# Retention and two MoE layers on one core: where raw weight tiles wait, and in which step a tile or a chunk's copy is handled

## The chip, the core and the metric

One core of a Trainium2 chip runs the kernel. The metric is the device time in microseconds of one execution; 1212.71 us is the median of 3 runs of the kernel before (1211.6 to 1213.98). The engines are TensorE (PE, with its weight loads as PEld), VectorE (DVE), ScalarE (ACT), GpSimd (POOL) and SyncE (SP, which here only issues transfers).

## The reference

```python
# retention: B, H, S, D = 4, 8, 768, 64
state = gamma * state + outer(k[t], v[t])      # per batch and head
y[t] = q[t] @ state / sqrt(D)
# x: 3072 tokens of 512 (all heads of a token side by side)
h = x @ w_in                                   # 512 -> 2048
P = a[0] + a[1]*h + a[2]*h**2 + a[3]*h**3
Q = 1 + abs(b[0])*abs(h) + abs(b[1])*h**2
x = (P / (Q + 1e-6)) @ w_out                   # 2048 -> 512
h = x @ w_in2
out = (h * clip(h + 3, 0, 6) / 6) @ w_out2
```

All is float32.

## The kernel before, in words

**Matmuls.** Each float32 operand is split into a high part that TensorE takes as it is and a low remainder, so each product is three passes: high by high, high by low, low by high. The 3072 tokens are 6 blocks of 512, the 2048 hidden columns 16 tiles of 128 (`f`). One step of the main loop (L657) is one block and one `f` of one layer: `emit_h` (L322) makes 12 matmuls into a PSUM tile `h`, and `emit_o` (L334) makes the 12 matmuls of the output for the step two before (`LAG`). There are 192 steps. Layer 0 (the rational function) begins with block 0, `f` 0 to 7 (steps 0 to 7, `CUT1`), then block 1 with all 16 `f` (steps 8 to 23), then block 0's other 8 (steps 24 to 31), then blocks 2 to 5.

**Between the matmuls.** For layer 0 each step holds, one step behind `h`, `s1_h` (ACT, L403 to 405), `s1_pq` (DVE, L411, 412, 415) and `s1_r` (ACT, L420 and 421), and two steps behind, `s1_g` (DVE, L426 to 428), `s_hi` (ACT, L433, the high part `gh`) and `s_lo` (DVE, L439, the low part `gl`). The output matmuls of a step wait for that step's `gh` and then its `gl`.

**Weights.** A weight tile is one job: 32 jobs for layer 0, in the order in which they are needed (`jobs`, L485). A job is a load of 512 KB by SP (`w_load`), a scaling on ACT (L116), three bit operations on DVE (`w_bits`, L124, 125, 128), the high part on ACT (L136), and the low part either by a POOL transfer that adds (jobs 3 to 25, with one more ACT copy, L140) or by a DVE subtraction (L148, jobs 26 to 31). `w_until(n)` (L500) says how many jobs are to be done after step n: a step does one or two until that number is reached. `w_ahead` (L509) issues loads as soon as a place is free. There are six places: two `raw` tiles and the four tiles in which the finished weights `wi14`, `wo14`, `wi15` and `wo15` will lie (`SPARE`); before, jobs from number 24 on may use the two `raw` tiles alone. Job 24 is `wo` of f = 11, and the last, 31, is `wo` of f = 15.

**Retention.** A block has 4 chunks of 128 tokens. `chunk_at` (L552) puts a chunk's parts into steps: the loads (SP, five transfers), `att_q` and `att_v` (DVE, L201 and 206), the scores (PE, L219), the mask (DVE, L228), the output `py` and the new state (PE, L250 to 276), and then `att_xh` (ACT, L306, or L301 for block 2, whose result goes through DRAM) and `att_evac` (DVE, L313 and 317). The lists `begin`, `before` and `after` say where in a step a part stands: `begin` ahead of `s1_g` and `s_hi`, `before` behind `s1_pq`, `after` behind the output matmuls. Block 1's chunks are worked in steps -1 to 7, block 2's (`VIA`) from step 8 on.

**Order.** Nothing is moved by a scheduler: each engine runs its instructions in the order in which the loop writes them, and waits in that order. SP's loads wait in their order too, each for its place.

```python
w_until:  4 + 2 * (n + 1) if n < CUT1 else 4 + 2 * CUT1 + n + 1 - CUT1
w_ahead:  rooms = [t for t in free if i < SPARE_TO or t not in SPARE]
w_first:  w_bits(job i); w_scale_next(i + 3); w_hi(job i)
loop:     emit_h, s1_h, begin, s1_g + s_hi, w_second, w_first,
          s1_pq with s_lo inside, s1_r, before, [w_second, w_first], w_ahead,
          emit_o, after
```

Of the kernel before, what the change touches and what calls it, by code (L numbers as in the profile page):

```python
# [18 lines left out]
VIA = 2  # L19
CUT1, CUT2 = 8, 8  # L20
LAG = 2
SUMS = ((3, 26), (32, 40))
EARLY_AT = 8
SPARE, SPARE_TO = ("wi14", "wo14", "wi15", "wo15"), 24
WARM = 3
Q_CONST = 1.0 + 1e-6
LN_SCALE = 2.0**16
# [4 lines left out]
def tile_retention_moe_moe2(  # L32
# [66 lines left out]
    def w_load(tag, kind, layer, f):  # L99
        src = ((w_in1, w_in2) if kind == "wi" else (w_out1, w_out2))[layer].bitcast(I32)  # L100
        raw = pair_tile(tag, f"r{kind}{layer}_{f}").bitcast(I32)
        if kind == "wi":
            nc.sync.dma_start(
                out=raw.rearrange("p (c f) -> p c f", c=KD),
                in_=src[:, f * 256 : (f + 1) * 256].rearrange("(c p) f -> p c f", p=128),
            )
        else:
            nc.sync.dma_start(out=raw, in_=src[f * 128 : (f + 1) * 128, :])
        raws[kind, layer, f] = raw.rearrange("p (n t) -> p n t", t=2)
# [212 lines left out]
    def emit_h(key):  # L322
        layer, blk, f = key
        ps = ps_h.tile([128, 512], F32, tag="h", name=f"h{layer}_{blk}_{f}")
        wh, wl = weights["wi", layer, f]
        xh, xl = xin[blk + layer * NBLK]
        pairs = ((wh, xh), (wh, xl), (wl, xh))
        for n, (i, c) in enumerate((i, c) for i in range(3) for c in range(KD)):
            w, x = pairs[i]
            cs = slice(c * 128, (c + 1) * 128)  # L330
            nc.tensor.matmul(ps, lhsT=w[:, cs], rhs=x[:, c, :], start=n == 0, stop=n == 3 * KD - 1)  # L331
        hps[key] = ps
# [41 lines left out]
    def emit_evac(layer, blk, f):  # L374
        earlier = partial.pop((layer, blk), None)
        for j, ps in enumerate(acc.pop((layer, blk))):
            scale = G_SCALE if layer == 0 else 1.0 / 6.0
            if earlier:
                o = earlier[j]
                nc.vector.scalar_tensor_tensor(out=o, in0=ps, scalar=scale, in1=o, op0=ALU.mult, op1=ALU.add)  # L380
            else:
                o = out_tile(layer, blk, j, f"o{layer}_{blk}_{f}_{j}")
                if layer == 0 or j % 2 == 0:
                    nc.scalar.activation(o, ps, AF.Copy, scale=scale)
                else:
                    nc.vector.tensor_scalar(out=o, in0=ps, scalar1=scale, scalar2=None, op0=ALU.mult)
            t0 = blk * NB + j * 128
            if layer == 0:
                to = x2_dram[blk][j]
            else:  # L390
                to = out[t0 : t0 + 128, :] if f == FT - 1 else part_dram[j]
            nc.sync.dma_start(out=to, in_=o)
# [31 lines left out]
    def s1_g(key):  # L424
        u, p, r = tm[key]
        nc.vector.scalar_tensor_tensor(out=u, in0=u, scalar=Q_CONST, in1=r, op0=ALU.add, op1=ALU.mult)  # L426
        nc.vector.scalar_tensor_tensor(out=p, in0=p, scalar=ab[:, 0:1], in1=r, op0=ALU.add, op1=ALU.mult)  # L427
        nc.vector.scalar_tensor_tensor(out=p, in0=u, scalar=-2.0 * LN_SCALE, in1=p, op0=ALU.add, op1=ALU.mult)  # L428
        tm[key] = p

    def s_hi(key):
        gh = g_p.tile([128, NB], F32R, tag="gh", name="gh" + "_".join(map(str, key)))
        nc.scalar.activation(gh, tm[key], AF.Copy)  # L433
        gsp[key] = gh

    def s_lo(key):
        gh = gsp[key]
        gl = g_p.tile([128, NB], F32R, tag="gl", name="gl" + "_".join(map(str, key)))
        nc.vector.tensor_tensor(out=gl, in0=tm.pop(key), in1=gh.bitcast(F32), op=ALU.subtract)  # L439
        gsp[key] = (gh, gl)  # L440
# [40 lines left out]
    def at_step(n):  # L481
        return steps[n] if 0 <= n < len(steps) else None


    jobs = []  # L485
    for layer in range(2):
        need = []
        for f in range(FT):
            n = min(at_of[layer, b, f] for b in range(NBLK))
            need += [(n, "wi", layer, f), (n + LAG, "wo", layer, f)]  # L490
        jobs += [j[1:] for j in sorted(need, key=lambda j: j[0])]
    NW = 2 * FT
    made = {"load": 0, "scale": 0, "bits": 0, "lo": 0}
    free = [*SPARE, "raw", "raw"]
# [5 lines left out]
    def w_until(n):  # L500

        if n < N1 - FT:
            return min(NW, 4 + 2 * (n + 1) if n < CUT1 else 4 + 2 * CUT1 + n + 1 - CUT1)
        m = n - N1
        if m < 0:
            return NW + (m + FT) // 2
        return min(2 * NW, NW + 7 + (135 * (m + 1) + 99) // 100 if m < CUT2 else NW + 11 + m)

    def w_ahead(lim):  # L509
        while made["load"] < lim:  # L510
            i = made["load"]
            rooms = [t for t in free if i < SPARE_TO or t not in SPARE]
            if not rooms:
                return
            held[i] = rooms[0]
            free.remove(rooms[0])
            w_load(held[i], *jobs[i])
            made["load"] += 1
# [8 lines left out]
    def w_first():  # L527
        i = made["bits"]
        if made["scale"] == i:
            w_ahead(i + 1)  # L530
            w_scale_next(i + 1)
        w_bits(*jobs[i])
        w_scale_next(i + 3)
        w_hi(*jobs[i])
        if by_dma(i):
            w_minus(*jobs[i])
        made["bits"] += 1
# [6 lines left out]
            made["lo"] += 1  # L544


    begin, before, after, begun = {}, {}, {}, []

    def put(where, n, fn, *args):
        where.setdefault(n, []).append((fn, *args))  # L550

    def chunk_at(blk, c, s, loads=None):  # L552
        if loads is not None:
            put(before, loads, att_load, blk, c)
        put(before, s - 1, att_q, blk, c)
        put(before, s - 1, att_v, blk, c)
        put(after, s, att_scores, blk, c)
        put(before, s + 1, att_mask, blk, c)
        put(after, s + 1, att_out, blk, c)
        put(begin, s + 2, att_xh, blk, c)  # L560
        put(before, s + 2, att_evac, blk, c)

    for c in range(CPB):
        chunk_at(1, c, 2 * c - 1, max(2 * c - 4, -1))
        chunk_at(VIA, c, CUT1 + 1 + 4 * c, CUT1 - 1 + 4 * c)
        for b in range(VIA + 1, NBLK):
            n0 = at_of[0, b - 1, 0] if b > VIA + 1 else 2 * FT
            chunk_at(b, c, n0 + 4 * c, n0 + 4 * c - 2)
    for key in (VIA, *range(NBLK, 2 * NBLK)):
        n = at_of[0, key, 0] if key < NBLK else at_of[1, key - NBLK, 0]  # L570
# [20 lines left out]
    att_load(0, 0, (3, 2))  # L591
    att_load(0, 1)
    w_ahead(1)
    att_load(0, 2)
    att_load(0, 3, (0, 4, 1, 3))
# [51 lines left out]
    att_evac(0, 3)  # L647
    w_second()
    w_first()
    for parts in (begin, before, after):  # L650
        for n in sorted(n for n in parts if n < 0):
            for fn, *args in parts.pop(n):
                if fn is not att_load:
                    begun.append((fn, *args))

    late = []
    for n in range(len(steps) + LAG):  # L657
        cur, k1, k2 = (at_step(n - i) for i in range(3))
        todo = w_until(n) - made["bits"]
        if cur:  # L660
            emit_h(cur)
        for fn, *args in begun:
            fn(*args)
        begun.clear()
        if k1:
            (s1_h, s2_h)[k1[0]](k1)
        for key in late:
            if key[:2] not in partial and key[0] == 0:
                emit_evac(*key)
        for fn, *args in begin.get(n, ()):  # L670
            fn(*args)
        if k2 and k2[0] == 0:
            s1_g(k2)
            s_hi(k2)
        elif k2:
            s_lo(k2)
        for key in late:
            if key[:2] in acc:
                emit_evac(*key)
        late.clear()  # L680
        while made["lo"] < made["bits"]:
            w_second()
        rest = (lambda: s_lo(k2)) if k2 and k2[0] == 0 else None
        if k1 and k1[0] == 1:
            if rest:
                rest()
            s2_g(k1)
            s_hi(k1)
        if todo > 0:
            w_first()  # L690
        if k1 and k1[0] == 0:
            s1_pq(k1, rest)
            s1_r(k1)
        if todo > 1:
            w_second()
        for fn, *args in before.get(n, ()):
            fn(*args)
        if n == N1 - FT:
            free += ["kv", "T"]
        if todo > 1:  # L700
            w_first()
        w_ahead(NW if n < N1 - FT else 2 * NW)
        if n == 1:
            w_scale_next(NW)
        o = at_step(n - LAG)
        if o:
            emit_o(o)
            if o[2] == ends[o][1]:
                late.append(o)
        for fn, *args in after.get(n, ()):  # L710
            fn(*args)
        if cur and cur[1:] == (0, FT - 1):
            sum_load(*cur[:2])
# [71 lines left out]
```

## Time and profile before

| | us |
|---|---|
| median of 3 runs | 1212.71 (1211.6 to 1213.98) |
| profiled execution, its own time | 1212.05 |
| its span, first to last instruction | 1210.1 |
| PE busy / DVE busy / ACT busy | 1158.3 / 805.6 / 624.5 |
| mean granted TensorE clock | 0.984 of full |

The profiled execution lies 0.66 us under the median. In the span, steps 0 to 191 begin with their first `h` matmul; step 8 begins at 105.55 us, step 23 at 230.42 us. A busy share of PE says little, since matmuls overlap; the distance from one step's first `h` matmul to the next one's is the measure of pace.

### The profile page before, as it was taken

The numbers are of one execution on the slowest core, as the hardware profiler recorded it, in microseconds if no ns is written. First come the engines' busy times: TensorE is split into PE (matmuls) and PEld (weight loads), VectorE is DVE, ScalarE is ACT, GpSimd is POOL, SyncE is SP. The second block draws the span as 40 slices with busy tenths as digits, with TensorE's granted clock in tenths as the row PEclk, the third lists the DMA queues.
The fourth block names the chain that finished last, engine by engine and source line by source line (L and its number), as shares of the span: only waits on it lengthen the run. The fifth ranks groups of instructions, "written<-read, shape, count | busy, mean of one in ns | idle before, by whom it ended". The sixth has DMA issues, their size and how long they took to land.

```text
span 1210.1 us, 15716 instructions
## 1 busy us (share of the span) xinstructions
PE 1158.3 (96%) x6022; PEld 937.0 (77%) x6022; DVE 805.6 (67%) x1250; ACT 624.5 (52%) x1017; POOL 27.6 (2%) x37
## 2 busy tenths in 40 slices
PE   7687798999999999999999999999999999999998
PEld 5565676788888888888777788888888888888886
DVE  6899789999888788887899997643332232322222
ACT  2577666676666666756787765433222222322222
POOL 0112000000000000000000000000000000000000
PEclk9889999999999999999999999999999999999999
DMA  9877543032111311213233454202100100100000
GB/s 334 261 181 189 152 126 101 27 131 79 45 44 44 103 63 44 79 44 110 62 87 83 121 176 139 87 1 87 61 9 1 61 9 1 61 9 1 35 1 35
DMA packets 59115, 99.42 MB, mean 82 GB/s; under 512 B 5280, under 2 KB 23840, under 8 KB 59040
## 3 DMA queue, kind: packets, MB, share of 16 engines
q1 hardware_dynamic: 54576, 90.29, 22.6%
q0 software_dynamic: 4464, 8.13, 4.1%
q8 instruction: 47, 0.77, 0.3%
q14 instruction: 28, 0.23, 0.1%
HBM read 74.54 MB, written 15.73 MB: 75 GB/s over the span
## 4 chain that ended last, share of the span: by engine, by line
PE 74%; DVE 5%; ACT 2%; issue 1%; ACTq 0%; DVEq 0%
PE h L331 36%; PE accA L355 18%; PE accB L355 18%; PE sc L219 1%; PE py L250 1%; DVE u L426 1%; DVE u L412 1%; DVE p L411 1%; DVE p L427 1%; PE py L276 1%; ACT r L420 0%; ACT r L421 0%; DVE p L415 0%; PE py L262 0%; DVE p L428 0%
## 5 line engine op out<-in xcount | busy, mean ns | idle before, releaser
L331 PE MATMUL h<-xh,wi 128*128 128x512 f32 x1536 | 419.7, 395 | 0.7 <-ACT xh L306 0.7
L331 PEld LDWEIGHTS h<-xh,wi 128*128 128x128 f32 x1536 | 288.4, 190 | 65.4 <-issue 3.3
L331 PE MATMUL h<-xl,wi 128*128 128x512 f32 x768 | 207.5, 392 | 0.0
L451 DVE SCALAR_TENSOR_TENSOR g<-r,h 128x512 f32<-128x512 f32 x96 | 66.0, 688 | 164.5 <-ACT r L445 164.0
L331 PEld LDWEIGHTS h<-xl,wi 128*128 128x128 f32 x768 | 145.5, 189 | 31.4
L445 ACT ACTIVATE r<-h,cst 128x512 f32<-128x512 f32 x96 | 65.9, 687 | 178.0 <-PE h L331 177.5
L439 DVE TENSOR_TENSOR gl<-g,gh 128x512 fp32r<-128x512 f32 x96 | 66.5, 692 | 112.3 <-ACT gh L433 112.3
L433 ACT ACTIVATE gh<-g 128x512 fp32r<-128x512 f32 x96 | 60.8, 633 | 150.5 <-PE accB L355 116.5
L355 PE MATMUL accA<-gh,wo 128*128 128x512 f32 x384 | 121.5, 398 | 12.4 <-ACT gh L433 12.3
L355 PE MATMUL accB<-gh,wo 128*128 128x512 f32 x384 | 120.7, 396 | 0.0
L355 PE MATMUL accB<-wo,gh 128*128 128x512 f32 x384 | 118.2, 389 | 0.0
L355 PE MATMUL accA<-wo,gh 128*128 128x512 f32 x384 | 118.2, 389 | 0.0
L355 PEld LDWEIGHTS accA<-gh,wo 128*128 128x128 f32 x384 | 71.7, 190 | 31.9 <-ACT gh L433 17.4
L403 ACT ACTIVATE p<-h,ab 128x512 f32<-128x512 f32 x96 | 74.3, 774 | 39.0 <-PE h L331 36.4
L420 ACT ACTIVATE r<-u,cst 128x512 f32<-128x512 f32 x96 | 69.2, 721 | 42.2 <-DVE u L412 42.2
L439 DVE TENSOR_TENSOR gl<-p,gh 128x512 fp32r<-128x512 f32 x96 | 65.9, 686 | 32.9 <-ACT gh L433 32.7
L355 PEld LDWEIGHTS accB<-gh,wo 128*128 128x128 f32 x384 | 73.7, 192 | 15.8
L355 PEld LDWEIGHTS accA<-wo,gh 128*128 128x128 f32 x384 | 72.1, 188 | 15.0
L355 PEld LDWEIGHTS accB<-wo,gh 128*128 128x128 f32 x384 | 72.1, 188 | 14.9
L433 ACT ACTIVATE gh<-p 128x512 fp32r<-128x512 f32 x96 | 60.7, 632 | 34.9 <-DVE p L428 34.9
L355 PE MATMUL accA<-gl,wo 128*128 128x512 f32 x192 | 64.9, 414 | 14.3 <-DVE gl L439 14.3
L355 PE MATMUL accA<-wo,gl 128*128 128x512 f32 x192 | 74.7, 389 | 0.0
(74 smaller groups left out, 1477.3 us busy)
## 6 DMA issues: line engine op xcount, KB each, us to landing
rwi<-in_moe_w_in_dram SPq DMA_DIRECT2D x32, 512.0 KB, 4.4
rwo<-in_moe_w_out_dram SPq DMA_DIRECT2D x32, 512.0 KB, 4.1
T<-in_qk_t_dram SPq DMA_DIRECT2D x48, 256.0 KB, 4.2
kv<-in_kv_dram SPq DMA_DIRECT2D x32, 256.0 KB, 4.5
x<-o SPq DMA_DIRECT2D x24, 256.0 KB, 2.2
xr<-x SPq DMA_DIRECT2D x24, 256.0 KB, 3.6
out_dram<-o SPq DMA_DIRECT2D x20, 256.0 KB, 2.1
wi<-rwi POOLq DMA_DIRECT2D x17, 256.0 KB, 4.8
```

The lines of the kernel that those rows point to most:

```text
L219: nc.tensor.matmul(banks[e][:, p * CH : (p + 1) * CH], lhsT=kT[rows, p, :], rhs=qT[rows, p, :], start=True, stop=True)
L250: nc.tensor.matmul(to(e, j, i), lhsT=vr[:, 2 * p + e, :], rhs=am[:, e * NP + p, :], start=j == 0, stop=first and j == 1, skip_group_check= ...
L276: nc.tensor.matmul(to(e, j, i), lhsT=state[rows, p * D : (p + 1) * D], rhs=qT[rows, p, :], start=False, stop=j == 1, skip_group_check=True,)
L331: nc.tensor.matmul(ps, lhsT=w[:, cs], rhs=x[:, c, :], start=n == 0, stop=n == 3 * KD - 1)
L355: nc.tensor.matmul(acc[layer, blk][j], lhsT=l, rhs=r, start=f == f0 and i == 0, stop=f == f1 and i == 2)
L403: nc.scalar.activation(p, h, AF.Identity, scale=ab[:, 3:4], bias=ab[:, 2:3])
L411: nc.vector.tensor_tensor(out=p, in0=p, in1=h, op=ALU.mult)
L420: nc.scalar.activation(r, u, AF.Ln, scale=1.0 / LN_SCALE, bias=ln_bias)
L433: nc.scalar.activation(gh, tm[key], AF.Copy)
L439: nc.vector.tensor_tensor(out=gl, in0=tm.pop(key), in1=gh.bitcast(F32), op=ALU.subtract)
L445: nc.scalar.activation(r, hps[key], AF.Relu, bias=three)
L451: nc.vector.scalar_tensor_tensor(out=g, in0=r, scalar=6.0, in1=h, op0=ALU.min, op1=ALU.mult)
```

## The change

Four things change. The four spare tiles may hold a raw tile of any job that lies at least three jobs ahead of the weight that will live there (so jobs up to 24, 26, 27 and 28 in `wi14`, `wi15`, `wo14` and `wo15`), where before it was jobs up to 23 in all four. From step 8 on, `w_until` asks for four jobs in five steps instead of one in each: steps 8 to 19 did 13 jobs (two in step 8), now steps 8 to 22 do them, with none in steps 13 and 18. For blocks 1 and 2 `att_xh` stands in a new list `middle`, behind `s_hi`. Block 2's loads, scores, mask and output stand one step earlier, its `att_xh` and `att_evac` in the same step as before.

```diff
--- before.py
+++ after.py
@@ -21,7 +21,7 @@
 LAG = 2
 SUMS = ((3, 26), (32, 40))
 EARLY_AT = 8
-SPARE, SPARE_TO = ("wi14", "wo14", "wi15", "wo15"), 24
+SPARE = ("wi14", "wi15", "wo14", "wo15")
 WARM = 3
 Q_CONST = 1.0 + 1e-6
 LN_SCALE = 2.0**16
@@ -500,7 +500,7 @@
     def w_until(n):
 
         if n < N1 - FT:
-            return min(NW, 4 + 2 * (n + 1) if n < CUT1 else 4 + 2 * CUT1 + n + 1 - CUT1)
+            return min(NW, 4 + 2 * (n + 1) if n < CUT1 else 4 + 2 * CUT1 + 4 * (n + 1 - CUT1) // 5)
         m = n - N1
         if m < 0:
             return NW + (m + FT) // 2
@@ -509,7 +509,7 @@
     def w_ahead(lim):
         while made["load"] < lim:
             i = made["load"]
-            rooms = [t for t in free if i < SPARE_TO or t not in SPARE]
+            rooms = [t for t in free if t not in SPARE or i + 3 <= jobs.index((t[:2], 0, int(t[2:])))]
             if not rooms:
                 return
             held[i] = rooms[0]
@@ -544,7 +544,7 @@
             made["lo"] += 1
 
 
-    begin, before, after, begun = {}, {}, {}, []
+    begin, middle, before, after, begun = {}, {}, {}, {}, []
 
     def put(where, n, fn, *args):
         where.setdefault(n, []).append((fn, *args))
@@ -557,12 +557,14 @@
         put(after, s, att_scores, blk, c)
         put(before, s + 1, att_mask, blk, c)
         put(after, s + 1, att_out, blk, c)
-        put(begin, s + 2, att_xh, blk, c)
+
+        s += blk == VIA
+        put(middle if blk <= VIA else begin, s + 2, att_xh, blk, c)
         put(before, s + 2, att_evac, blk, c)
 
     for c in range(CPB):
         chunk_at(1, c, 2 * c - 1, max(2 * c - 4, -1))
-        chunk_at(VIA, c, CUT1 + 1 + 4 * c, CUT1 - 1 + 4 * c)
+        chunk_at(VIA, c, CUT1 + 4 * c, CUT1 - 2 + 4 * c)
         for b in range(VIA + 1, NBLK):
             n0 = at_of[0, b - 1, 0] if b > VIA + 1 else 2 * FT
             chunk_at(b, c, n0 + 4 * c, n0 + 4 * c - 2)
@@ -647,7 +649,7 @@
     att_evac(0, 3)
     w_second()
     w_first()
-    for parts in (begin, before, after):
+    for parts in (begin, middle, before, after):
         for n in sorted(n for n in parts if n < 0):
             for fn, *args in parts.pop(n):
                 if fn is not att_load:
@@ -674,6 +676,8 @@
             s_hi(k2)
         elif k2:
             s_lo(k2)
+        for fn, *args in middle.get(n, ()):
+            fn(*args)
         for key in late:
             if key[:2] in acc:
                 emit_evac(*key)
```

SP's queue around the load of job 24 (`rwo_11`; `rwi_f` and `rwo_f` are raw tiles, `T_1`, `tq_1` and `kv_1` the loads of block 2's second chunk, `x_0` block 0's partial result going to DRAM). Before:

```order
L302 DMA x_via<-xf_0_1227 128x4x128
L194 DMA T_1_1251<-in_qk_t_dram 128x512
L194 DMA tq_1_1253<-in_tables_dram 128x512
L194 DMA T_1_1251<-in_qk_t_dram 128x512
L194 DMA kv_1_1252<-in_kv_dram 128x512 x2
L108 DMA rwo_11_1259<-in_moe_w_out_dram 128x1024
L103 DMA rwi_13_1315<-in_moe_w_in_dram 128x4x256
```

Now:

```order
L108 DMA rwo_9_886<-in_moe_w_out_dram 128x1024
L103 DMA rwi_11_888<-in_moe_w_in_dram 128x4x256
L108 DMA rwo_10_980<-in_moe_w_out_dram 128x1024
L103 DMA rwi_12_982<-in_moe_w_in_dram 128x4x256
L108 DMA rwo_11_1036<-in_moe_w_out_dram 128x1024
L103 DMA rwi_13_1100<-in_moe_w_in_dram 128x4x256
L392 DMA x_0_101<-o_0_7_0_1158 128x512
```

The load of job 24 stands ahead of the partial result's store and of the second chunk's loads, where it stood behind both; the next job's load comes up with it.

DVE in steps 12 to 14 (`p` and `u` with a step's `f` behind; `gl_1_2` is the low part for block 1, f = 2). Before, from the end of step 12's `s1_g`:

```order
L428 SCALAR_TENSOR_TENSOR p_2_1223<-u_2_1222,p_2_1223 128x512
L124 TENSOR_SCALAR rwo_11_1259<-rwo_11_1259 128x512
L125 SCALAR_TENSOR_TENSOR rwo_11_1259<-rwo_11_1259 128x512
L128 SCALAR_TENSOR_TENSOR rwo_11_1259<-rwo_11_1259 128x512
L411 TENSOR_TENSOR p_3_1288<-p_3_1288,h_1_3_1208 128x512
L412 SCALAR_TENSOR_TENSOR u_3_1287<-s_3_1286,babs,u_3_1287 128x512
L439 TENSOR_TENSOR gl_1_2_1307<-p_2_1223,gh_1_2_1295 128x512
L415 SCALAR_TENSOR_TENSOR p_3_1288<-p_3_1288,ab,h_1_3_1208 128x512
```

Now, from the end of step 13's `s1_g`:

```order
L428 SCALAR_TENSOR_TENSOR p_3_1290<-u_3_1289,p_3_1290 128x512
L411 TENSOR_TENSOR p_4_1353<-p_4_1353,h_1_4_1275 128x512
L412 SCALAR_TENSOR_TENSOR u_4_1352<-s_4_1351,babs,u_4_1352 128x512
L439 TENSOR_TENSOR gl_1_3_1365<-p_3_1290,gh_1_3_1360 128x512
L415 SCALAR_TENSOR_TENSOR p_4_1353<-p_4_1353,ab,h_1_4_1275 128x512
L228 TENSOR_TENSOR T_1_1191<-sc_1_1329,tab 128x1024
L426 SCALAR_TENSOR_TENSOR u_4_1352<-u_4_1352,r_4_1368 128x512
L427 SCALAR_TENSOR_TENSOR p_4_1353<-p_4_1353,ab,r_4_1368 128x512
L428 SCALAR_TENSOR_TENSOR p_4_1353<-u_4_1352,p_4_1353 128x512
L124 TENSOR_SCALAR rwo_11_1036<-rwo_11_1036 128x512
L125 SCALAR_TENSOR_TENSOR rwo_11_1036<-rwo_11_1036 128x512
L128 SCALAR_TENSOR_TENSOR rwo_11_1036<-rwo_11_1036 128x512
```

Job 24's three bit operations stood in step 12; they now stand in step 14, and step 13 has none. The mask of block 2's second chunk, now in step 13, stood in step 14.

ACT in step 11 (`xf_0` is the copy of block 2's first chunk). Before:

```order
L403 ACTIVATE p_2_1223<-h_1_2_1117,ab 128x512
L404 ACTIVATE s_2_1221<-h_1_2_1117 128x512
L405 ACTIVATE u_2_1222<-h_1_2_1117,ab 128x512
L301 ACTIVATE xf_0_1227<-py_0_1183 128x512
L433 ACTIVATE gh_1_1_1233<-p_1_1132 128x512
L136 ACTIVATE wi_12_1239<-rwi_12_980 128x512
L140 ACTIVATE wi_12_1239<-wi_12_1239 128x512
L420 ACTIVATE r_2_1247<-u_2_1222,cst 128x512
```

Now:

```order
L403 ACTIVATE p_2_1230<-h_1_2_1139,ab 128x512
L404 ACTIVATE s_2_1228<-h_1_2_1139 128x512
L405 ACTIVATE u_2_1229<-h_1_2_1139,ab 128x512
L433 ACTIVATE gh_1_1_1237<-p_1_1154 128x512
L301 ACTIVATE xf_0_1239<-py_0_1114 128x512
L116 ACTIVATE rwo_11_1036<-rwo_11_1036 128x512
L136 ACTIVATE wo_10_1247<-rwo_10_980 128x512
L140 ACTIVATE wo_10_1247<-wo_10_1247 128x512
L420 ACTIVATE r_2_1255<-u_2_1229,cst 128x512
L421 ACTIVATE r_2_1255<-r_2_1255 128x512
```

The copy `xf_0` stands behind `gh` instead of ahead of it, and the scaling of job 24 (L116) now stands here, three steps ahead of its bit operations.

## Rows read from the trace of the kernel before

**Rows 1.** Page, the span in 40 equal slices: busy tenths of PE and of DVE.

```profile
PE   7687798999999999999999999999999999999998
...
DVE  6899789999888788887899997643332232322222
```

**Rows 2.** Busy time by stretch: us, then busy us (count) per engine, clock, DMA share.

```profile
105.50:230.40 124.90, 106.66 (x601) 81.79 (x600) 110.03 (x175) 80.93 (x135) 7.01 (x9) 0.93 0.42 118
230.40:582.20 351.80, 351.80 (x2076) 286.84 (x2073) 302.48 (x465) 230.24 (x372) 0.00 (x0) 1.00 0.21 70
```

**Rows 3.** Timeline of PE, layer 0: start us, us, instruction; steps 26, 27, 44 and 46.

```profile
246.88 1.07 PE L331 MATMUL h<-xh,wi 128*128 128x512 f32 x4
...
252.31 1.07 PE L331 MATMUL h<-xh,wi 128*128 128x512 f32 x4
...
355.12 1.07 PE L331 MATMUL h<-xh,wi 128*128 128x512 f32 x4
...
369.50 1.19 PE L331 MATMUL h<-xh,wi 128*128 128x512 f32 x4
```

**Rows 4.** Waits of DVE from 107.6 to 226.8 us: total, times, longest.

```profile
DVE rwo L124 <- DMA rwo<-in_moe_w_out_dram: 6.0, 2, 5.5
DVE rwo L125 <- ACT rwo L116: 2.8, 5, 1.0
DVE rwi L125 <- ACT rwi L116: 2.3, 3, 1.0
DVE u L426 <- ACT r L421: 1.6, 5, 0.8
DVE gl L439 <- ACT gh L433: 0.6, 2, 0.3
```

**Rows 5.** Timeline of DVE, step 8.

```profile
107.64 0.68 DVE L426 SCALAR_TENSOR_TENSOR u<-u,r 128x512 f32<-128x512 f32 x1
...
109.63 0.53 DVE L124 TENSOR_SCALAR rwi<-rwi 128x512 int32<-128x512 int32 x1
...
111.53 0.68 DVE L411 TENSOR_TENSOR p<-p,h 128x512 f32<-128x512 f32 x1
...
114.05 0.69 DVE L201 TENSOR_TENSOR T<-T,tq 128x512 f32<-128x512 f32 x1
...
115.26 0.43 DVE L124 TENSOR_SCALAR rwo<-rwo 128x512 int32<-128x512 int32 x1
```

**Rows 6.** Timeline around step 12: SP's load, DVE, PE; the bracket is idle time before.

```profile
139.57 0.39 SPq L108 DMA_DIRECT2D rwo<-in_moe_w_out_dram  x1
...
147.23 0.43 DVE L124 TENSOR_SCALAR rwo<-rwo 128x512 int32<-128x512 int32 x1 [5.53 <-DMA rwo<-in_moe_w_out_dram]
...
151.26 1.22 PE L355 MATMUL accA<-gl,wo 128*128 128x512 f32 x2 [5.11 <-DVE gl L439]
...
153.13 1.91 PE L331 MATMUL h<-xh,wi 128*128 128x512 f32 x4
```

**Rows 7.** Timeline of DVE and PE where steps 20 and 23 begin.

```profile
209.98 0.69 DVE L426 SCALAR_TENSOR_TENSOR u<-u,r 128x512 f32<-128x512 f32 x1
210.16 1.08 PE L331 MATMUL h<-xh,wi 128*128 128x512 f32 x4
...
226.81 0.68 DVE L426 SCALAR_TENSOR_TENSOR u<-u,r 128x512 f32<-128x512 f32 x1
...
230.42 1.19 PE L331 MATMUL h<-xh,wi 128*128 128x512 f32 x4
```

**Rows 8.** Timeline of ACT and PE, step 5.

```profile
83.03 0.61 ACT L306 ACTIVATE xh<-py 128x512 fp32r<-128x512 f32 x1
...
84.21 0.74 PE L355 MATMUL accA<-gh,wo 128*128 128x512 f32 x2 [2.56 <-ACT gh L433]
```

**Rows 9.** DMA issues: count, KB each, median us from issue to landing.

```profile
rwo<-in_moe_w_out_dram SPq DMA_DIRECT2D x32, 512.0 KB, 4.1
...
wi<-rwi POOLq DMA_DIRECT2D x17, 256.0 KB, 4.8
```

## The prediction

> **What bounds the kernel now.** I read the page's slices first. PE is under nine tenths busy in six of the first seven slices and then in the last alone, while DVE stands at eight or nine tenths in five of those seven [rows 1]. The busy times by stretch say it in numbers: from step 8 to step 23 (124.9 us) PE is busy for 106.66 us at a mean clock of 0.93 and DVE for 110.03, while in the stretch behind it PE has no idle time at all [rows 2]. So behind step 23 the matmuls set the pace, and this change, which touches nothing there, can't shorten it. What PE needs is read from two distances: 5.44 us from step 26 to step 27, and 14.38 us for the two steps 44 and 45, in which one chunk's scores and output lie, so 3.50 us for a chunk [rows 3]. The 15 steps from 8 to 22 with four chunks need 15 x 5.44 + 4 x 3.50 = 95.6 us of PE. They take 124.9. The 29.3 us between are what there is to win in this stretch.
>
> Who takes them? DVE. Its instructions stand nearly end to end there; the view of its waits finds 13.3 us of waiting in the 119.17 us from its step 8 (107.64) to its step 23 (226.81): 6.0 for a raw tile to land, 5.1 for the scaling of a raw tile on ACT, 1.6 for the reciprocal, 0.6 for `gh` [rows 4, 5, 7]. The rest, 105.9 us, is work. The reader is to see that PE's own gaps (5.11 us in step 12 for one [rows 6]) are the shadow of DVE's.
>
> **The change part by part.** *Moved work on DVE.* In step 8, a step's own work is 1.99 us (L426 to L124) and 2.52 us (L411 to L201), a weight tile costs 1.90, a chunk's two products 1.21 [rows 5]. Both kernels do 13 tiles, 15 steps and four chunks on DVE between step 7 and step 22. The spreading therefore buys no DVE time by itself: tiles leave steps 8 to 19 and reappear in 20 to 22. Two things cross the stretch's ends. The first chunk's two products go into step 7 and push step 8 back by 1.21 us, which the stretch then does not hold: nought in sum. The last tile's subtraction (L148) goes behind the start of step 23, a gain of 0.6 us (half of those two products, which have its shape), and step 23 has room for it: 1.99 + 2.52 + 0.6 is under PE's 5.44.
>
> *The wait for the raw tile.* Job 24 was loaded from 139.57 us, when a `raw` tile came free, and DVE could begin on it only at 147.23: 7.66 us, of which DVE stood still for 5.53 [rows 6]. In the changed order this load stands ahead of the second chunk's loads, two steps or more ahead of step 14 where it is used. Jobs 24 to 29 all load by step 13. I take the whole 5.53 as gone, and the 0.47 us of the second wait for a landing [rows 4].
>
> *The waits for the scaling.* They come from the same cause: a tile that lands one step before its use can't be scaled ahead, so DVE waits within the step, 5.1 us in eight places. With early loads the scaling of jobs 24 to 29 stands steps ahead. Jobs 30 and 31 still have only the `raw` tiles, load one step ahead and wait: 5.1 us in eight waits is 0.64 each, so 1.3 for both.
>
> *What stays or comes.* DVE's wait for the reciprocal (L426) shows in steps with nothing between L415 and L426; with the chunks one step up, that is seven steps (8, 12, 14, 16, 18, 20, 22; step 10 stands below). Nearest rows: 1.6 us in five waits, one of them 0.8 [rows 4], so 0.2 each for the rest: 1.4 us. In step 10 ACT makes four copies of block 0's partial result ahead of `gh`; the mask that covered this on DVE has gone to step 9. I take the longest such wait, 0.8 us, there, and 0.3 for `gh` [rows 4]. Left in all: 1.3 + 1.4 + 0.8 + 0.3 = 3.8 us. The bounds are 1.4 (the reciprocal alone) and 7.8 (all the old waits but the 5.53).
>
> *The copies behind `gh`.* In step 5 `xh` stood ahead of `gh` on ACT and held it for half a microsecond, and PE had been idle for 2.56 us when it began [rows 8]. The swap brings those matmuls 0.5 us forward in steps 3, 5 and 7. I cost it at nothing: DVE is not held by them in steps 2 to 8, where it is full, and it sets the next step. If that cover were gone, it would be 3 x 0.5 us of gain. For block 2, `py` comes a step earlier and the copy stands behind `gh`, so `gh` no longer waits for `py` there; DVE waited for `gh` only 0.6 us in all [rows 4], so again next to nothing.
>
> *Queues.* On SP the five loads of block 2's chunks are issued one step earlier, in the first case ahead of two raw tiles (jobs 20 and 21) that are used two or more steps later; at 0.39 us for an issue [rows 6] that is 2 us, less than half a step. POOL's sums keep their order, in more steps; a sum lands in 4.8 us [rows 9], and the tile that it frees is written as a finished weight at least three jobs later, three steps of 5.44 us or more, so ACT's write doesn't wait.
>
> **The sum.** DVE's step 23 begins at 226.81 - 13.3 - 0.6 + 3.8 = 216.7 us. PE's first `h` matmul comes 0.2 us behind DVE's step where DVE leads (209.98 and 210.16) [rows 7]; I take 0.3, so 217.0 against 230.42 before, when PE was already 3.6 us behind DVE and at its own pace. The gain is 13.4 us. PE's 95.6 us fit into the 111.5 that are left, so it doesn't take the bound over. The rest of the program is the same: 1212.05 - 13.4 = 1198.65 for the profiled execution, which lay 0.66 under the median of the runs shown, so 1199.3.
>
> **TensorE's clock.** After the 5.11 us gap four matmuls of `h` take 1.91 us instead of 1.07, so they ran at 1.2 GHz instead of 2.4 [rows 3, 6]. A mean clock of 0.93 over 124.9 us [rows 2] means some 17.5 us at the low level, and half of that, 8.7 us, is what full clock would have saved PE. I add nothing for it, since DVE, not PE, ends the steps. The Trainium skill ("TensorE: Matmul & The Clock Gate", "HAM oscillation — how this bites in real kernels") counts half of the throttled time as penalty in wall time; by that the 8.7 us would come on top and the sum be 1190.6. The same section warns that a loop that waits in every pass pays the throttling in every pass.
>
> **Rivals.** (a) *The last loads come late.* Jobs 30 and 31 each wait as job 24 did: 5.5 us in step 21, perhaps again in step 22. For: one `raw` tile, one step ahead, a load that once took 7.66 us. Against: no chunk's loads are in the queue then, the median landing is 4.1 us [rows 9] and a step with a tile lasts about 7. Time: 1204.8 with one, 1210.3 with both. (b) *The loads aren't early at all*, since SP takes them in order behind a wait: the 5.53 remain and only the rest is saved: 1204.8. Against: the order shown. (c) *The clock is given back in time as well*: 1190.6. For: PE's half speed is real. Against: PE had idle time in that stretch all the same; what it saves it waits. (d) *The other side: the clock stays low.* PE now waits a little for DVE in each of 15 steps instead of long in a few. If it stays at 1.2 GHz in much of the stretch, PE becomes the bound: it decides below a mean clock of 95.6/111.5 = 0.86, and the kernel is slower than before below 95.6/124.9 = 0.77; at 0.70 the stretch takes 136.6 us, 1224. For: step 12's aftermath. Against: 0.93 with far longer gaps.
>
> **How the numbers follow.** Forecast 0.83; (a) 0.08, half of it with one wait; (b) 0.04; (c) 0.01; (d) 0.04, three quarters of it slower than before. The bounds of the waits left give 1196.9 (1.4 us) to 1203.3 (7.8 us). With (a) once and (b) the range is 1196 to 1205. A measurement here tells 0.2%, some 2.4 us, from no change. Faster by more: all but (d) and the doubled half of (a), most of which is too near to tell: 0.93; the same 0.04; slower 0.03.
>
> **What would show it.** Right: DVE's waits in steps 8 to 22 sum to 2 to 5 us, none over 1.5, none for a raw tile's landing; step 23 begins near 217 us; the mean clock from step 8 to step 23 is at 0.95 or more; everything behind it is only shifted. Wrong: a DVE wait of over 3 us there, a wait of ACT's L136 for a raw tile's sum, or `h` of step 23 more than 1 us behind DVE's step.

## The result and the profile after

The changed kernel takes 1200.59 us (median of 4 runs, 1199.67 to 1203.01) against 1212.68 for the kernel before. The ratio is 0.9903 with a 95% interval of 0.9885 to 0.992, a gain of 9.7 to 13.9 us. The forecast was 1199.3 in a range of 1196 to 1205. The profiled execution took 1200.7 us, 1198.8 of it in the span, where before it was 1212.05 and 1210.1.

The page's slices, PE and DVE, answer to [rows 1]:

```profile
PE   7687999999999999999999999999999999999998
...
DVE  6899999999878888788899987633332232322222
```

PE is now under nine tenths in four of the first seven slices instead of six. The busy times by stretch, which answer to [rows 2]; the last cut lies 11.3 us earlier than there, which is the difference of the spans:

```profile
105.70:218.00 112.30, 101.36 (x602) 77.66 (x601) 106.23 (x170) 79.90 (x133) 7.03 (x9) 0.98 0.44 120
218.00:570.90 352.90, 352.09 (x2074) 286.59 (x2073) 305.78 (x471) 231.39 (x375) 0.00 (x0) 1.00 0.21 70
```

The first stretch is 12.6 us shorter, with the same number of matmuls (602 and 601), so PE's work is the same and its idle time fell from 18.2 to 10.9 us. The mean clock rose from 0.93 to 0.98. The second stretch is 1.1 us longer than before, and PE, which had no idle time in it, now has 0.8 us. DVE's waits between the starts of its steps 8 and 23 (109.1 to 218) answer to [rows 4]:

```profile
DVE u L426 <- ACT r L421: 3.2, 8, 1.7
DVE gl L439 <- ACT gh L433: 0.8, 1, 0.8
DVE rwo L125 <- ACT rwo L116: 0.7, 2, 0.3
```

Of 13.3 us of waiting, 4.7 are left. The wait for a landing is gone, the one for the scaling is nearly gone, and the one for the reciprocal has doubled. Half of the last is one wait, at the start of DVE's step 11; its cause lies in step 10. The timeline there, of SP, ACT and DVE:

```profile
124.64 4.33 SPq L392 DMA_DIRECT2D x<-o  x4
...
124.96 0.62 ACT L384 ACTIVATE o<-accB 128x512 f32<-128x512 f32 x1
...
128.03 0.60 ACT L384 ACTIVATE o<-accB 128x512 f32<-128x512 f32 x1 [2.44 <-DMA x<-o]
128.52 0.62 ACT L433 ACTIVATE gh<-p 128x512 fp32r<-128x512 f32 x1
...
129.17 0.69 DVE L439 TENSOR_TENSOR gl<-p,gh 128x512 fp32r<-128x512 f32 x1 [0.77 <-ACT gh L433]
...
132.19 0.69 DVE L426 SCALAR_TENSOR_TENSOR u<-u,r 128x512 f32<-128x512 f32 x1 [1.67 <-ACT r L421]
```

ACT copies block 0's partial result in four pieces, and there are three output tiles. The fourth copy waits 2.44 us until the first piece's store has landed; `gh` and the reciprocal stand behind it on ACT, and DVE waits 0.77 and 1.67 us for them. Before, the copies came later and the same copy waited 0.35 us:

```profile
128.08 0.60 ACT L384 ACTIVATE o<-accB 128x512 f32<-128x512 f32 x1 [0.35 <-DMA x<-o]
```

The end of the stretch answers to [rows 7], and two steps more are shown (DVE, PE and ACT):

```profile
217.76 0.69 DVE L426 SCALAR_TENSOR_TENSOR u<-u,r 128x512 f32<-128x512 f32 x1 [0.20 <-ACT r L421]
217.99 1.08 PE L331 MATMUL h<-xh,wi 128*128 128x512 f32 x4
...
223.49 1.08 PE L331 MATMUL h<-xh,wi 128*128 128x512 f32 x4
...
225.99 0.63 ACT L465 ACTIVATE xh<-xr 128x512 fp32r<-128x512 f32 x1 [1.07 <-DMA xr<-x_via]
...
227.19 0.73 PE L355 MATMUL accA<-gh,wo 128*128 128x512 f32 x2 [0.81 <-ACT gh L433]
...
230.05 1.07 PE L331 MATMUL h<-xh,wi 128*128 128x512 f32 x4
```

Step 23 begins 12.4 us earlier than before (217.99 against 230.42), and PE now stands 0.23 us behind DVE instead of 3.6. Step 24 takes 6.56 us instead of 5.44. There ACT waits for the first piece of block 2's input to come back from DRAM (L465), `gh` stands behind that on ACT, and PE behind `gh`. The rest of the program has not moved: from step 25 to the end of the span it is 968.75 us after (1198.8 - 230.05) and 968.66 before.

### The profile page after: what moved, and what is told of

The parts are those of the page before. It is cut to its first block, busy times and chain, and to the rows that moved or that the text cites. A ratio compares the mean times of both kernels' runs of the same rounds, so it can differ in the third digit from the quotient of the medians.

```text
span 1198.8 us, 15717 instructions
## 1 busy us (share of the span) xinstructions
PE 1152.7 (96%) x6022; PEld 931.1 (78%) x6022; DVE 804.7 (67%) x1250; ACT 624.3 (52%) x1017; POOL 27.5 (2%) x37
## 4 chain that ended last, share of the span: by engine, by line
PE 77%; DVE 13%; DMA 4%; ACT 3%; issue 2%; SPq 0%; DVEq 0%; ACTq 0%
PE h L331 37%; PE accA L355 18%; PE accB L355 18%; DVE p L411 1%; DMA rwo<-in_moe_w_out_dram 1%; DVE u L426 1%; DVE p L427 1%; PE sc L219 1%; PE py L250 1%; DVE u L412 1%; DMA T<-in_kv_dram 1%; DVE p L415 1%; DVE rwo L125 1%; DVE p L428 1%; DVE rwi L125 1%
## 5 line engine op out<-in xcount | busy, mean ns | idle before, releaser
L355 PE MATMUL accB<-wo,gl 128*128 128x512 f32 x192 | 74.7, 389 | 0.0
```

Source lines behind the costliest of these rows:

```text
L355: nc.tensor.matmul(acc[layer, blk][j], lhsT=l, rhs=r, start=f == f0 and i == 0, stop=f == f1 and i == 2)
```

## The experiments

In all fourteen profiled executions the time from step 25 to the span's end is 968.6 to 968.9 us. A span is therefore the place where step 8 begins, plus the stretch from step 8 to step 25, plus 968.7. The first of these scatters from one execution to the next: step 8 begins between 104.53 and 108.52 us. So beside each median stands the stretch, from the first `h` matmul of step 8 to that of step 25 in the profiled execution; it leaves the start's scatter out. How well a stretch repeats is known from one kernel alone, the one after, profiled twice (124.35 and 124.48 us). Ratios are to the kernel before on the same chip, whose median is 1212.85 us beside experiments 1 to 4, 1214.00 beside 5 to 8 and 1213.26 beside 9 to 12.

| kernel | median us | ratio (95%) | step 8 | step 25 | stretch |
|---|---|---|---|---|---|
| before | 1212.68 | | 105.55 | 241.44 | 135.89 |
| after | 1200.59 | 0.9903 (0.9885 to 0.992) | 105.70 | 230.05 | 124.35 |
| 1: spare places alone | 1204.70 | 0.9932 (0.9912 to 0.9952) | 106.31 | 234.24 | 127.93 |
| 2: fewer tiles per step alone | 1207.41 | 0.9955 (0.9938 to 0.9973) | 105.79 | 236.88 | 131.09 |
| 3: chunks and copies alone | 1207.39 | 0.9961 (0.995 to 0.9972) | 104.53 | 236.08 | 131.55 |
| 4: before, gaps filled | 1212.91 | 1.0004 (0.9992 to 1.0016) | 107.21 | 244.13 | 136.92 |
| 5: before, all chunk loads last | 1210.96 | 0.9976 (0.9965 to 0.9988) | 105.84 | 240.75 | 134.91 |
| 6: after, no spare places | 1203.74 | 0.9913 (0.9897 to 0.993) | 106.90 | 234.00 | 127.10 |
| 7: after, old tiles per step | 1205.91 | 0.9936 (0.9915 to 0.9956) | 104.85 | 232.88 | 128.03 |
| 8: after, old chunks and copies | 1199.07 | 0.9886 (0.9864 to 0.9909) | 108.52 | 233.41 | 124.89 |
| 9: after, `tq` tile | 1199.65 | 0.989 (0.9877 to 0.9904) | 107.02 | 229.22 | 122.20 |
| 10: as 9, later reading back | 1197.44 | 0.9876 (0.9861 to 0.9892) | 105.23 | 226.16 | 120.93 |
| 11: before, later chunks' loads last | 1209.33 | 0.9962 (0.9949 to 0.9974) | 107.14 | 239.01 | 131.87 |
| 12: after, again | 1201.02 | 0.99 (0.9887 to 0.9914) | 105.39 | 229.87 | 124.48 |

### One part alone: 1, 2 and 3

The kernel before with the new rule for the spare tiles:

```diff
-SPARE, SPARE_TO = ("wi14", "wo14", "wi15", "wo15"), 24
+SPARE = ("wi14", "wi15", "wo14", "wo15")
...
-            rooms = [t for t in free if i < SPARE_TO or t not in SPARE]
+            rooms = [t for t in free if t not in SPARE or i + 3 <= jobs.index((t[:2], 0, int(t[2:])))]
```

> The kernel before with the rule for the four spare tiles alone; pace of the tiles and chunks as before. Theory A (VectorE's waits and the balance of its work set the stretch from step 8 to 23): the wait for job 24's landing and six of eight waits for a scaling go, about 9.5 us, so VectorE reaches step 20 near 200.5 instead of 209.98; but steps 20 to 22 hold no tile and go at TensorE's pace (20.3 us), so step 23 begins near 221 and the time is 1203 (1201.5 to 1205). Rival B (the spare tiles are the whole gain): 1200.6, as the changed kernel.

Measured: 1204.70 us, as theory A has it; rival B, the ratio of the changed kernel, lies outside the interval. DVE waits for no landing any more, and 1.4 us for the scaling (two waits) instead of 5.1. From step 20 on PE paces the steps, as before the change: step 23's first matmul comes at 223.23, 3.6 us behind DVE's start of the step (219.61). One wait grew, that for `gh`, from 0.6 us in two waits [rows 4] to 2.0 in one (108.4 to 219.6):

```profile
DVE gl L439 <- ACT gh L433: 2.0, 1, 2.0
```

It is the one of step 10 that the changed kernel has too, where it is 0.8. Early loads are not its only cause: in experiment 3, which has none, DVE waits for `gh` there too (0.75 us).

The kernel before with fewer tiles per step:

```diff
-            return min(NW, 4 + 2 * (n + 1) if n < CUT1 else 4 + 2 * CUT1 + n + 1 - CUT1)
+            return min(NW, 4 + 2 * (n + 1) if n < CUT1 else 4 + 2 * CUT1 + 4 * (n + 1 - CUT1) // 5)
```

> The kernel before with the slower pace of tiles behind step 8 alone. Theory A: job 24 now has one and a half steps between the free raw tile and its use, so the wait of 5.5 us goes too, while some six waits for a scaling stay (4 us); VectorE reaches step 23 near 219.5, and the last chunk's mask and output still stand in step 22, which puts TensorE's step 23 near 222: 1204.5 (1202.5 to 1207). Rival B (the spare tiles are the whole gain): 1212.7, nothing gained.

Measured: 1207.41 us, 0.4 above theory A's range; rival B (nothing gained) falls. Job 24's wait is gone, since the job is used two steps later, but DVE waits 4.43 us for job 26 instead, in step 16 (SP and DVE):

```profile
162.12 0.38 SPq L194 DMA_DIRECT2D T<-in_qk_t_dram  x1
...
164.53 0.38 SPq L108 DMA_DIRECT2D rwo<-in_moe_w_out_dram  x1
...
171.72 0.43 DVE L124 TENSOR_SCALAR rwo<-rwo 128x512 int32<-128x512 int32 x1 [4.43 <-DMA rwo<-in_moe_w_out_dram]
```

The load of that job stands behind the five loads of a chunk, and 7.2 us pass from its issue to its use. In [rows 6] it was 7.66 us for job 24, which also stood behind five such loads.

The kernel before with block 2's chunks a step earlier and the copies behind `gh`:

```diff
-        put(begin, s + 2, att_xh, blk, c)
+        s += blk == VIA
+        put(middle if blk <= VIA else begin, s + 2, att_xh, blk, c)
...
-        chunk_at(VIA, c, CUT1 + 1 + 4 * c, CUT1 - 1 + 4 * c)
+        chunk_at(VIA, c, CUT1 + 4 * c, CUT1 - 2 + 4 * c)
```

> The kernel before with block 2's chunks one step earlier and the copies of blocks 1 and 2 behind gh alone. Theory A: ScalarE's waits for the attention output end, but VectorE was not held by them: 1212 (1210.5 to 1213.5). Rival C (gh held by a copy that waits was a cost): 1209 or less.

Measured: 1207.39 us. Theory A, the prediction's reasoning, fails: this part, costed at next to nothing, is worth 5.5 us by the medians and 4.3 in the stretch when it is alone. The time is one that rival C allowed, but its reason does not hold: DVE waits 0.75 us for `gh` from step 8 to step 23, where it was 0.6. Its waits for landings fell from 6.0 to 1.5 us. The trace shows where it comes from (SP and DVE, steps 10 to 12):

```profile
129.47 0.37 SPq L194 DMA_DIRECT2D T<-in_qk_t_dram  x1
...
137.94 0.33 SPq L108 DMA_DIRECT2D rwo<-in_moe_w_out_dram  x1
...
142.26 0.43 DVE L124 TENSOR_SCALAR rwo<-rwo 128x512 int32<-128x512 int32 x1 [0.30 <-DMA rwo<-in_moe_w_out_dram]
```

The chunk's loads were issued 8 us ahead of job 24's instead of right in front of it. The load still waits for its `raw` tile until 137.94, but it then lands within 4.3 us, and DVE waits 0.30 instead of 5.53 us. So what made job 24 late was, for the most part, the five transfers in front of it; experiments 5 and 11 try that by itself.

### The cause of the 5.53 us by itself: 5 and 11

The kernel before, with SP's order alone changed: a block-2 chunk's loads behind the step's tile load. In experiment 5 for all chunks, in 11 for all but the first.

```diff
-            put(before, loads, att_load, blk, c)
+            put(after if blk == VIA else before, loads, att_load, blk, c)         # 5
+            put(after if blk == VIA and c else before, loads, att_load, blk, c)   # 11
```

> The kernel before with one thing changed: the five loads of block 2's chunk are issued behind the step's tile load on SyncE's queue instead of ahead of it; plan, raw tiles and copies stay. Theory A (the 5.53-us wait for job 24 comes from its load standing behind the chunk's copy and five loads on SyncE's queue): the wait falls below 0.6 us, the time is about 1207 us (1205.5 to 1209). Rival B (only a raw tile that comes free earlier helps): the wait stays above 4 us, 1212.7 (1211.5 to 1214).

> The kernel before with the loads of block 2's second and later chunks behind the step's tile load on SyncE's queue, the first chunk's ahead of it as they were. Theory: job 24's 5.53-us wait falls below 0.6, and the 3.9 us that the first chunk's late loads cost when they were moved too do not come: 6 us below the kernel before of this call (4.5 to 7). Rival (another load of the chunk becomes late in its place): 3 us below it or less.

Measured: 1210.96 us (2.9 us less than before by the ratio, 1.5 to 4.2) and 1209.33 us (4.6 us less, 3.2 to 6.2). Job 24's wait is gone in both, which is what theory A of the first and the theory of the second said. The time of 5 lies between the ranges of its two theories; the gain of 11 lies at the low end of its theory's by the ratio, and below it by the medians (3.9). In 11 (SP and DVE):

```profile
139.25 0.37 SPq L302 DMA_DIRECT2D x_via<-xf  x1
139.78 0.38 SPq L108 DMA_DIRECT2D rwo<-in_moe_w_out_dram  x1
140.26 0.40 SPq L194 DMA_DIRECT2D T<-in_qk_t_dram  x1
...
144.23 0.42 DVE L124 TENSOR_SCALAR rwo<-rwo 128x512 int32<-128x512 int32 x1
```

The load is issued at 139.78 (139.57 in [rows 6]), and DVE begins on it 4.45 us later without a wait, where it took 7.66 us. The tiles are the same; the five transfers in front of it are gone. Of the 5.53 us, 3.2 are this shorter time. Counted from step 8 the load is also issued 1.4 us earlier, and DVE comes to it 0.9 us later.

In the kernel before, SP's order held the load back ahead of its issue too. In experiment 3, with the same places, the load waits for POOL's transfer out of job 22's `raw` tile. Before, that transfer was issued at 130.68 us and landed 3.7 us later, so the place was free near 134.4, 5.2 us ahead of the load. SP stood at the store of the first chunk's copy, which ACT made only at 136.00, and then issued the store and the five loads (POOL, ACT and SP):

```profile
130.68 0.86 POOL L146 DMA_DIRECT2D wo<-rwo  x1 [7.05 <-DVE p L415]
136.00 0.60 ACT L301 ACTIVATE xf<-py 128x512 f32<-128x512 f32 x1 [2.60 <-PE py L276]
136.63 0.37 SPq L302 DMA_DIRECT2D x_via<-xf  x1
137.10 0.45 SPq L194 DMA_DIRECT2D T<-in_qk_t_dram  x1
```

In 5 the wait moved (SP and DVE, steps 8 and 9):

```profile
110.64 0.37 SPq L103 DMA_DIRECT2D rwi<-in_moe_w_in_dram  x1
111.06 0.82 SPq L194 DMA_DIRECT2D T<-in_qk_t_dram  x1
111.94 0.50 SPq L194 DMA_DIRECT2D tq<-in_tables_dram  x1
...
117.09 0.69 DVE L201 TENSOR_TENSOR T<-T,tq 128x512 f32<-128x512 f32 x1 [2.69 <-DMA tq<-in_tables_dram]
119.02 0.69 DVE L206 TENSOR_TENSOR kv<-kv,tab 128x512 f32<-128x512 f32 x1 [1.23 <-DMA kv<-in_kv_dram]
```

The first chunk's loads now stand behind a tile load that is held until its place is free at 110.64, so they are issued some 9.5 us later than before, and DVE waits 3.92 us for them. That took back most of the 5.53. In 11 this wait does not come, and the stretch is 4.0 us shorter; a wait for `gh` in step 11 grew from 0.3 to 1.3 us there, and one of 0.6 for a landing in step 13 is new.

### The clock by itself: 4

The kernel before with 47 extra matmuls in the gaps of five steps:

```diff
+FILL = {8: (8, 0), 9: (6, 0), 12: (0, 20), 16: (0, 9), 17: (0, 4)}
...
+        ahead, between = FILL.get(at_of[key] + LAG, (0, 0))
+
+        def fill(count, x):
+            for _ in range(count):
+                nc.tensor.matmul(acc[layer, blk][0], lhsT=wh[:, 0:128], rhs=x, start=False, stop=False)
+
+        fill(ahead, xin[1][0][:, 0, :] if ahead else None)
         for i, j in parts:
+            if (i, j) == (2, 0):
+                fill(between, gh)
```

> The kernel before with 47 more matmuls that fill TensorE's gaps in steps 8, 9, 12, 16 and 17 (8, 6, 20, 9 and 4 of 512 columns, added into one bank of the output sum of block 0 or 1, so that part of the output holds extra products). Theory A: the granted clock of steps 8 to 22 rises from 0.93 to 0.96 or more, and the time stays, 1212.5 (1211.5 to 1214.5). Rival D (half clock costs time there): the 8.7 us that full clock saves TensorE come back in part, 1208 or less, down to 1204.

Measured: 1212.91 us, ratio 1.0004. The busy times from step 8 to step 23:

```profile
107.21:233.12 125.91, 113.56 (x649) 87.40 (x647) 109.99 (x175) 80.93 (x135) 6.98 (x8) 0.97 0.41 111
```

The clock rose from 0.93 to 0.97, by as much as the whole change brought bar 0.01, and the stretch did not become shorter: it is 1.0 us longer. DVE's work and its other waits are as before (the waits for landings took 6.8 us instead of 6.0), so the filling did not eat up a gain. Theory A holds, and rival D, by which the clock would have been worth time, falls.

### The change without one part: 6, 7 and 8

> The kernel after without raw tiles in the spare places. Theory A (the parts remove the same wait, each of them): what is lost is the waits for the scaling and the py matmuls that are bunched at the end, about 2.5 us: 1203 us (1201.5 to 1205), no wait for a landing over 1 us in steps 8 to 22. Rival B (the parts add up, each is worth what it gave alone, 8.1 us for this one): 1208.7.

> The kernel after with the old number of tiles per step behind the eighth. Theory A: the wait for job 24 stays away, but steps 20 to 22 hold the last tiles' matmuls and TensorE paces them (20.3 us for the three with the spare places alone): 1204 us (1202 to 1206). Rival B (the parts add up, 5.4 us for this one): 1206.

> The kernel after with block 2's chunks left where they were, and the copies ahead of gh. Theory A (its gain alone was the same job-24 wait, which the other parts have removed): at most 2 us are lost, 1202 us (1200 to 1204), and step 24 loses its 1-us wait for the chunk read back. Rival B (the parts add up, 5.5 us for this one): 1206.

Each is the kernel after with one of the three diffs above taken back. Without the spare places: 1203.74 us, theory A; rival B's 1208.7 is far off. No wait for a landing came back; that for the scaling did (108 to 232 us, 0.7 us in the changed kernel):

```profile
DVE rwo L125 <- ACT rwo L116: 3.9, 5, 1.4
```

With the old number of tiles per step: 1205.91 us, at the edge of A's range and on rival B's number, so the median does not decide. The trace does: the wait for job 24 stays away, and the three steps 20 to 22 take 20.7 us of PE, where the theory said 20.3:

```profile
201.27 1.07 PE L331 MATMUL h<-xh,wi 128*128 128x512 f32 x4
...
222.00 1.07 PE L331 MATMUL h<-xh,wi 128*128 128x512 f32 x4
```

DVE has begun its step 23 at 218.24 there, 3.8 us ahead of PE. The prediction had counted PE's need over the whole stretch, which fits; in its last three steps it does not fit unless tiles' work on DVE is left for them.

With the old chunks and copies: 1199.07 us, below theory A's range; by the medians nothing is lost. The stretch is 124.89 us against 124.35 and 124.48, so this part, worth 4.3 us there alone, is worth half a microsecond at most on top of the other two, too little to be sure of. It is a small remainder of larger terms. With the part, DVE takes 1.2 us less from its step 8 to its step 23 (108.65 instead of 109.88) and PE stands 1.7 us less behind it at the end, but DVE's step 8 begins 1.3 us later behind PE's and step 24, which takes 5.44 us without the part, is 1.1 us longer. The profiled execution without the part is the slowest of the four (1203.93, the others 1198.4 to 1199.3), and it began step 8 at 108.52 us, 2.8 us behind the changed kernel's.

### What is left: 9, 10 and 12

```diff
-        if j == KD - 1 and layer * NBLK + blk >= NBLK - 2:
+        if j == KD - 1 and (layer * NBLK + blk >= NBLK - 2 or (layer, blk) == (0, 0)):      # 9, 10
...
-                at, lag = n - 9 + c + 2 * (c > 1), 1
+                at, lag = n - 9 + c + 2 * (c > 1), 1 + (key == VIA and c == 0)             # 10
```

> The kernel after, with block 0's fourth partial result copied into the free tq tile. Theory: the 0.77 and 1.67 us that VectorE waits in steps 10 and 11 come from the fourth copy's wait for its output tile, so they fall to about 0.3 together, and the time to 2.0 us below the kernel after of this call (1 to 2.5). Rival (the loads that were issued earlier hold VectorE or TensorE up anyway): within 0.7 us of it.

> As the run before, and the reading back of block 2's first piece one step later. Theory: the 0.81-us gap of TensorE and the 1.07-us wait of ScalarE in step 24 go too, step 24 takes 5.5 us: 3 us below the kernel after of this call (2 to 3.6). Rival (the piece is then late in step 25): 2 us below it, as the run before.

> The kernel after, unchanged, on the chip of the three other runs: 1200.6 us (1198.5 to 1203), 12 us below the kernel before; step 24 again 6.5 us long, VectorE's waits in steps 10 and 11 again 2.4 us; the start of step 0 differs from 28.76 by up to 2.5 us, by what the first loads take.

Measured on one chip: 1201.02 us for the kernel after, 1199.65 with the fourth copy in the free tile, 1197.44 with the later reading back as well: 1.4 and 3.6 us less, in the stretch 2.3 and 3.6. Both theories hold. Since the runs of the first (1198.16 to 1201.27 us) overlap those of the kernel after, its gain rests on the stretch and on the waits. The kernel after repeated as expected: step 24 took 6.63 us, DVE's two waits in steps 10 and 11 took 2.5, and step 0 began at 27.28. DVE's waits from 106 to 232 us, of the kernel after on this chip:

```profile
DVE u L426 <- ACT r L421: 3.5, 9, 1.7
DVE gl L439 <- ACT gh L433: 1.5, 2, 0.8
DVE rwo L125 <- ACT rwo L116: 0.6, 2, 0.3
```

With the fourth copy in the `tq` tile:

```profile
DVE u L426 <- ACT r L421: 2.1, 9, 0.3
DVE gl L439 <- ACT gh L433: 0.7, 1, 0.7
DVE rwo L125 <- ACT rwo L116: 0.6, 2, 0.3
```

With both:

```profile
DVE u L426 <- ACT r L421: 2.3, 10, 0.3
DVE rwo L125 <- ACT rwo L116: 0.6, 2, 0.3
```

The first edit takes the 1.67 and the 0.83 of steps 10 and 11 away. The second takes the 0.7 of step 24, whose length falls to 5.47 us. The runs of the last version (1196.98 to 1199.15 us) all lie under those of the kernel after (1199.81 to 1201.64), so it beats both kernels.

## Why the prediction was right, and where it was not

**The bound: right.** The gain is for the most part DVE's waiting time. The stretch from step 8 to step 25 became 11.5 us shorter, DVE's waits up to step 23 8.6 us shorter, and the 1.8 us of work that the prediction let leave at the ends (the first chunk's products, the last subtraction) did leave: DVE's step 23 begins 108.65 us behind its step 8, 103.95 of it work, instead of 105.9. As forecast, the products come back as a later start of DVE's step 8 (1.3 us), and PE, 3.6 us behind DVE before and 0.2 after, adds 3.4 us. Step 23 began at 217.76 on DVE and 217.99 on PE; 216.7 and 217.0 were forecast.

**The clock: right.** Experiment 4 gave the clock back alone and gained nothing. The prediction's 17.5 us at the low level would by that clock be 7.6 (0.97 over 125.9 us). The Trainium skill ("TensorE: Matmul & The Clock Gate", "HAM oscillation — how this bites in real kernels") counts half of the throttled time as time lost, which would make the difference worth about 5 us, an estimate from that page's rule. The trace disagrees with it here: the measured ratio allows a gain of 1 us at most. Rivals (c) and (d) fall with it; the mean clock after is 0.98.

**The wait for job 24: right size, the cause half seen.** All 5.53 and the 0.47 us went, as the sum had it. The step that failed is "job 24 was loaded from 139.57 us, when a `raw` tile came free". The place was free 5.2 us earlier, near 134.4, and SP's order held the load. The prediction named the new order, and in rival (a) the chunk's loads in the queue, but it put the delay down to the place and gave the five issues a price of 2 us, for two other jobs alone. Experiments 3 and 11 show the transfers' part: with five chunk loads just ahead of it on SP's queue (the kernel before and experiment 2) a tile load needed 7.2 to 7.7 us until DVE could use it, and with none ahead 4.5 us or less, issued at nearly the same place in the stretch. The Trainium skill ("DMA: Bandwidth & Descriptors", "Two DMAs through the same engine are not ordered") says that descriptors in one queue of a DMA engine start in order; the runs agree.

Each of the three parts removes this wait by itself, the second at the price of the one for job 26. Alone they shorten DVE's waits for landings by 6.0, 1.5 and 4.4 us, 11.9 in all, where 6.0 are to be had. So the parts alone gain 8.0, 4.8 and 4.3 us in the stretch, 17.1 in all, and together 11.5; and each of them, taken back, costs only 2.8, 3.7 and 0.5.

**The moved chunk and the copies behind `gh`: costed at nothing, right on top of the other parts (0.5 us at most in experiment 8), wrong alone (4.3 us in experiment 3).** The copies' and the chunks' shares were not tried apart. In steps 3, 5 and 7 the swap of the copies shows no gain beyond the scatter: from step 0 to step 8 the seven kernels with the old copies take 77.1 to 79.1 us and the seven with the new ones 76.9 to 78.3.

**Tiles per step: half right.** The spreading buys DVE no work, as said. But it buys time at the end of the stretch, which the prediction got only by taking PE's need as evenly spread: without it PE paces steps 20 to 22 (experiment 7).

**The waits left: 4.7 us, 3.8 forecast.** The scaling of jobs 30 and 31 cost 0.7 instead of 1.3; the reciprocal outside step 11 cost 3.2 - 1.7 = 1.5 (1.4 forecast). The mis-sized term is step 10: 0.8 and 0.3 were taken, 2.44 measured. The prediction saw the four copies ahead of `gh` but not that they have three tiles, so that the fourth waits for a store; experiment 9 shows it. One of these waits, 1.67 us, is above the 1.5 that the prediction allowed as the longest.

**"The rest of the program is the same": wrong by 1.1 us.** The piece of block 2 that is read back one step ahead of its use landed late before the change too, and ACT waited for it in step 24:

```profile
236.09 0.63 ACT L465 ACTIVATE xh<-xr 128x512 fp32r<-128x512 f32 x1 [0.77 <-DMA xr<-x_via]
```

But PE was then 3.6 us behind DVE, and step 24 took 5.44 us all the same. Now PE is 0.2 us behind, and the wait, 1.07 us, reaches it. It stands behind the stretch in which waits were counted; experiment 10 takes it away. The profiled execution was forecast at 1198.65 and took 1200.7, 2.05 us more; this step's 1.12 and step 10's 1.34 (2.44 less the 1.1 forecast), less 0.6 that the scaling did not take, and the 0.15 by which step 8 began later than before, make 2.0 of it.

**Rivals (a) and (b)** did not come: no job waits for its landing.

## What to carry to other kernels

When a load is late, look first at what stands right ahead of it on its queue, and whether its place was not free long before: here turning round six issues cured the same wait as other places for tiles, fewer tiles per step or earlier chunks did, so that the gains of the parts did not add up. When a stretch gets faster, list what was just in time in it and in the first steps behind it, or late under cover of another engine's lag (a store that frees one of three tiles for a fourth copy, a piece read back one step ahead): each 1 to 2 us lost was such a transfer, and a free tile or one step more won it back. Where a program's start scatters by microseconds, compare the changed stretch by its own rows.

## What was not expected of the hardware

The place where step 8 begins scatters by 4.0 us over fourteen profiled executions (104.53 to 108.52), though most of the changed parts work behind it, while the 968.7 us behind step 25 repeat to 0.3 us. The first `h` matmul of step 0 lies between 26.38 us (experiment 3) and 31.41 (experiment 8), the two that also have the first and the last step 8. It is not the chip: on each of the three chips of the experiments step 0 scatters by 3.2 to 4.4 us. The DMA engines are busy for 0.95 and 0.93 of the first 26 us in these two, and move 330 and 320 GB/s:

```profile
0.00:26.00 26.00, 16.82 (x246) 12.54 (x246) 17.39 (x26) 5.21 (x8) 0.33 (x6) 1.00 0.95 330
```

```profile
0.00:26.00 26.00, 18.98 (x198) 13.82 (x198) 14.12 (x22) 4.93 (x7) 0.33 (x6) 0.87 0.93 320
```

So the difference is there before any changed instruction runs, in the first loads; why they differ was not tried.
